# Chunk 5's product with w1 as seven block products, the tail's last product in two PSUM tiles, and a new order of steps

## The chip, the cores and the metric

The kernel runs on one core of one Trainium2 chip. The metric is the device time of one execution in microseconds (us). The core has five engines that run their own queues: TensorE (PE in the profile: matmuls, with PEld for its weight loads), VectorE (DVE), ScalarE (ACT), GpSimd (POOL) and SyncE (SP, which here only issues DMAs). Matmul results land in PSUM, eight banks of 512 float32 columns on 128 partitions; VectorE and ScalarE read them from there.

## The reference

Eight batches, eight heads, 576 tokens, 64 columns a head. An attention without a score matrix comes first, then a feed-forward block that multiplies two products:

```python
def _attn_ref(q, k, v):
    q_s = q - np.max(q, axis=-1, keepdims=True)
    q_s = np.exp(q_s)
    q_s = q_s / (np.sum(q_s, axis=-1, keepdims=True) + 1e-09)
    k_s = k - np.max(k, axis=2, keepdims=True)
    k_s = np.exp(k_s)
    k_s = k_s / (np.sum(k_s, axis=2, keepdims=True) + 1e-09)
    kv = np.einsum('bhsd,bhse->bhde', k_s, v)
    return np.einsum('bhsd,bhde->bhse', q_s, kv).astype(np.float32)

def _moe_ref(x, w1, w2, w3, w_out):       # x: 4608 x 512
    a = x @ w1                            # 512 x 1024
    b = x @ w2
    h = a * b @ w3                        # 1024 x 1024
    return (h @ w_out).astype(np.float32) # 1024 x 512
```

## The kernel before

The kernel folds w3 and w_out into one matrix W3O (1024 x 512) at its start, so that a chunk of tokens needs three products: with w2, with w1, and of their elementwise product `ab` with W3O.

**Chunks.** Chunk c (0 to 7) holds 512 of batch c's 576 tokens; chunk 8 holds the remaining 64 tokens of all eight batches (512 again). For each batch, `attention(b)` plans the softmax steps of k (`kmx`, `cba`, `cbx`, `cb`, `ksub`, `kexp`) and of q (`qmx`, `qsub`, `qexp`, `qsm`, `qeps`, `qrc`, `qn`), the copy of v to float16 (`vc`), the small product k'v (`kv`, read out by `kve`, `kvr`, `kv2`), a DMA transpose of q (`qd`), and the product that gives x transposed (`xm.b.0` and `xm.b.1` for the chunk, `xt` for the 64 other tokens). `xs.b.p.i` and `xts` move x from PSUM to SBUF. A name's first number is the batch or chunk; in `up`, `vp` and `vk` the first number is 0 for w1 and 1 for w2.

**Products with w1 and w2.** In chunks 0 to 5 an `up` step is a group of matmuls that fills one PSUM tile of the ring `pab` (four tiles): four matmuls of 512 columns (chunks 2 to 5), or eight of 256 (chunks 0 and 1). `bs` copies w2's result to SBUF, `ab` multiplies w1's result from PSUM with it (VectorE). In chunks 6 to 8 (the list `UPS`) each product is cut into 2 x 2 blocks and done with seven block products in place of eight: `vp.one.c.g.i`, i from 1 to 7, g for one of two halves of the columns, four matmuls of 256 columns each (`gate`, L923). They need sums of blocks: of the weights (`wd`, `gate_sum`) and of x (`xd`, `x_sum`); partial results are copied out (`vk`, `gkept`), and the four blocks come together in `bs` (w2), `as` and `ab` (w1). `UP1`, an empty list here, names chunks in which w1 alone is done that way; the code for it is there.

**Product with W3O.** In chunks 2 to 8 (the list `SEVEN`) it is done with seven block products too: `sp.c.i` (`product`, L1009), eight matmuls of 256 columns each, with sums of `ab` (`sa`, `sums_of`) and of W3O (`sT`), three copies (`kept`), and the output blocks `os.c.11`, `os.c.12`, `os.c.21`, `os.c.22` (`block`, L1033). Block products 2, 1 and 7 take a tile each from the ring `po` (two tiles), in chunk 8 from `pab`; 6, 5 and 3 add to 1's tile, 4 to 7's. `st` stores a block by a DMA on SP's queue (`store_block`, L1044). In chunk 8 (the list `FINE`) block product 4 is cut into `sp.8.40` and `sp.8.4`, each with one half of the tile, and the last block is added and stored in halves (`os.8.210`, `os.8.21`, `st.8.210`, `st.8.21`).

**Order.** There is no scheduler at run time. `ORDER` is a list of all steps, written out in the file; `Plan.run` (L48) emits them in that order, and each engine works off its own steps in that order, waiting for semaphores where data or a buffer is late. `PICKS` says for steps that can run on two engines which one does it. Large elementwise steps that read SBUF alone (`ksub`, `qsub`, `qn`, `sa`, `sT`, `wd`, `xd`, `ab` from SBUF, and `vc` on GpSimd) are marked as steps of a port: where the list goes from one engine to the other among them, `run` adds a wait, so that VectorE and GpSimd take turns on them in the order of the list. The loads of q, k and v from batch 2 on stand in SP's queue with the stores and the DMA transposes. v of batches 2 to 7 uses one input buffer (`turn_of`); the other one holds the weight sums of w1 later.

A step that takes a tile of a ring must stand behind the steps that free the tile's last holder (in `Plan.run`):

```python
ring, n = fifo[s["takes"]], self.rings[s["takes"]]
for old in range(len(ring) - n, len(ring) - n + s["slots"]):
    assert old < 0 or done.issuperset(given[ring[old]]), name
```

## Time and profile before

| | |
|---|---|
| median of 3 runs | 231.06 us (231.03 to 231.07) |
| the profiled execution | 231.18 us, its span 229.4 us |
| TensorE busy, granted clock | 220.8 us (96%), 0.997 |
| VectorE busy | 202.3 us (88%) |
| ScalarE busy | 146.3 us (64%) |
| GpSimd busy | 144.0 us (63%) |

The span goes from the first to the last instruction of the profiled execution; 1.8 us of its time lie outside. A row of a timeline gives start, length, engine, line, operation, output and inputs, and in brackets how long the engine had been idle and what ended that. Matmuls are pipelined, and their ends are modelled: the step from one start to the next is what a group costs, its length is longer. A row of a list of groups gives busy time, mean duration in ns, and the idle time before them. Tiles that share a buffer appear under the buffer's name: `v` in the tail is an output tile, `w` a block sum.

### The profile page before, as it was taken

Reading aid. Unit: us, or ns where it says so; the run is one execution under the profiler, and the core shown is the slowest. Engines: PE = TensorE matmul, PEld = TensorE weight load, DVE = VectorE, ACT = ScalarE, POOL = GpSimd, SP = SyncE. Lnnn points to the kernel's source line nnn. Section 1 sums busy time; section 2 is a strip of 40 time slices with the busy share of each in tenths; the row PEclk is TensorE's granted clock in tenths of the full one; section 3 lists DMA queues with packets and bytes.
Section 4 is the critical chain, followed back from the end, with each engine's and each line's share of the span. In section 5 each row is a group of like instructions: output and inputs, shape, how many; then the busy total and the mean of one; then the engine's idle time right before and its main releaser. Section 6 shows DMA issues by size and latency. Waiting matters only on the chain.

```text
span 229.4 us, 5579 instructions
## 1 busy us (share of the span) xinstructions
PE 220.8 (96%) x2239; PEld 149.1 (65%) x2239; DVE 202.3 (88%) x312; ACT 146.3 (64%) x277; POOL 144.0 (63%) x93
## 2 busy tenths in 40 slices
PE   7789999999999999999999999999999999999993
PEld 2345558865857644445666665664788788888882
DVE  1997769989896999999999799899989999899982
ACT  0536855479963999959947988448568453244431
POOL 8233247919999997984895894643199335729200
PEclk9999999999999999999999999999999999999998
DMA  6999999999999979999993867872804420041447
GB/s 202 220 309 213 293 261 264 315 381 294 398 307 208 376 275 238 299 237 275 294 366 101 165 137 193 324 140 46 184 1 91 95 62 1 3 91 38 102 95 225
DMA packets 42201, 46.56 MB, mean 203 GB/s; under 512 B 17088, under 2 KB 29888, under 8 KB 42176
## 3 DMA queue, kind: packets, MB, share of 16 engines
q1 hardware_dynamic: 34640, 34.48, 54.6%
q0 software_dynamic: 7536, 11.73, 21.9%
q8 instruction: 17, 0.28, 0.5%
q14 instruction: 8, 0.07, 0.1%
HBM read 38.80 MB, written 9.44 MB: 210 GB/s over the span
## 4 chain that ended last, share of the span: by engine, by line
PE 68%; DMA 20%; POOL 5%; DVE 3%; issue 2%; ACT 1%; POOLq 0%; DVEq 0%
PE pab L850 27%; PE po L1023 16%; PE pg L938 9%; PE pab L938 7%; DMA q<-in_q_dram 7%; DMA k<-in_k_dram 6%; DMA w1sb<-in_moe_w_dram 5%; PE pab L1023 3%; PE po L872 2%; DMA qT<-en 2%; POOL en L656 2%; POOL q L624 2%; PE pkv L579 2%; PE xm L704 1%; DVE qr L637 1%
## 5 line engine op out<-in xcount | busy, mean ns | idle before, releaser
L850 PE MATMUL pab<-x,w1sb 128*128 128x256 f16 (+1 forms) x256 | 49.5, 326 | 0.1
L850 PE MATMUL pab<-x,w2sb 128*128 128x256 f16 (+1 forms) x256 | 49.5, 326 | 0.0
L554 POOL TENSOR_TENSOR k<-k,cb 128x1152 f32<-128x1152 f32 x13 | 34.1, 2631 | 14.5 <-DVE w L1007 8.7
L850 PEld LDWEIGHTS <-w1sb 128*128 128x128 f16 x256 | 24.5, 98 | 14.9 <-issue 0.4
L850 PEld LDWEIGHTS <-w2sb 128*128 128x128 f16 x256 | 24.3, 98 | 15.1 <-issue 1.1
L865 DVE TENSOR_TENSOR ab<-pab,bsb 128x512 f16<-128x512 f32 x48 | 31.8, 676 | 1.7 <-ACT bsb L365 1.2
L624 POOL TENSOR_TENSOR q<-q,qm 128x1280 f32<-128x1280 f32 (+1 forms) x13 | 27.8, 2144 | 4.7 <-issue 2.3
L365 ACT CAST bsb<-pab 128x512 f16<-128x512 f32 x37 | 21.7, 586 | 12.5 <-PE pab L850 12.1
L656 POOL TENSOR_TENSOR en<-eq,qr 128x1024 f16<-128x1024 f16 (+1 forms) x12 | 25.3, 2123 | 6.0 <-ACT bsb L365 5.0
L619 DVE TENSOR_REDUCE qm<-q 128x20 f32<-128x1280 f32 (+1 forms) x16 | 21.3, 1340 | 3.7 <-DMA q<-in_q_dram 3.7
L637 DVE TENSOR_REDUCE qr<-eq 128x20 f32<-128x1280 f16 (+1 forms) x16 | 21.4, 1341 | 1.1 <-ACT eq L632 1.0
L632 ACT ACTIVATE eq<-q 128x1280 f16<-128x1280 f32 (+1 forms) x16 | 18.6, 1167 | 5.4 <-DVE q L624 3.9
L1023 PEld LDWEIGHTS <-w 128*128 128x128 f16 x192 | 18.6, 98 | 4.1 <-issue 0.4
L531 DVE TRANSPOSE_TENSOR_REDUCE kt<-k 128x72 f32<-128x2304 f32 x8 | 20.6, 2570 | 0.3 <-DMA k<-in_k_dram 0.3
L365 ACT COPY q<-pg 128x512 f32<-128x512 f32 x19 | 10.8, 586 | 13.9 <-PE pg L938 7.7
L1023 PEld LDWEIGHTS <-ab 128*128 128x128 f16 x168 | 16.4, 98 | 4.3 <-issue 1.0
L562 ACT ACTIVATE ek<-k 128x1152 f16<-128x1152 f32 x16 | 18.4, 1167 | 0.0
L1023 PE MATMUL po<-w 128*128 128x256 f16 x144 | 18.0, 273 | 0.0
L1007 POOL TENSOR_TENSOR w<-ab 128x1024 f16<-128x1024 f16 x5 | 10.6, 2123 | 9.7 <-PE pg L938 3.7
L500 PE MATMUL po<-wosb,w3T 128*128 128x512 f16 x64 | 15.3, 379 | 0.6 <-DMA wosb<-in_moe_w_out_dram 0.4
L872 PE MATMUL po<-W3O,ab 128*128 128x512 f16 x64 | 15.2, 379 | 0.0
L365 ACT CAST v<-v 128x1152 f16<-128x1152 f32 x12 | 13.6, 1155 | 1.1 <-DMA v<-in_v_dram 1.0
(145 smaller groups left out, 425.4 us busy)
## 6 DMA issues: line engine op xcount, KB each, us to landing
out_dram<-osb SPq DMA_DIRECT2D x56, 128.0 KB, 2.5
q<-in_q_dram SPq DMA_DIRECT2D x5, 1152.0 KB, 8.0
v<-in_v_dram SPq DMA_DIRECT2D x5, 1152.0 KB, 7.6
k<-in_k_dram SPq DMA_DIRECT2D x4, 1152.0 KB, 10.4
k<-in_k_dram POOLq DMA_DIRECT2D x3, 1152.0 KB, 14.2
v<-in_v_dram POOLq DMA_DIRECT2D x1, 1152.0 KB, 13.5
q<-in_q_dram SPq DMA_DIRECT2D x2, 576.0 KB, 6.5
k<-in_k_dram SPq DMA_DIRECT2D x2, 576.0 KB, 5.4
```

The costliest lines, as they stand in the source:

```text
L365: return [(nc.scalar.copy if eng == "ACT" else engine[eng].tensor_copy)(out=out, in_=in_)]
L531: dve.tensor_reduce(out=st["kt", b].rearrange("p h j e -> p (h j e)"), in_=kb.rearrange("p h j (e c) -> p (h j e) c", c=QD), axis=AX.X, op ...
L554: return [engine[eng].tensor_tensor(out=kb[:, two(hp), :, :], in0=kb[:, two(hp), :, :], in1=st["cb", b][:, two(hp), None, :].broadcast_to( ...
L619: dve.tensor_reduce(out=st["qm", b][:, :, j], in_=qb[:, :, j, :], axis=AX.X, op=ALU.max)
L624: return [engine[eng].tensor_tensor(out=qb[:, :, j, :], in0=qb[:, :, j, :], in1=st["qm", b][:, :, j, None].broadcast_to([P, HH, n, D]), op ...
L637: dve.tensor_reduce(out=st["qr", b][:, :, slice(*PARTS[p])], in_=st["eq", b, p], axis=AX.X, op=ALU.add)
L656: return [engine[eng].tensor_tensor(out=st["en", b][:, j, :, :].rearrange("p j h d -> p h j d"), in0=st["eq", b, p], in1=st["qr", b][:, :, ...
L850: nc.tensor.matmul(st["p", one, c, sub, u][:, a * (t1 - t0):(a + 1) * (t1 - t0)], lhsT=w[:, ct, fb * P:(fb + 1) * P], rhs=x()[:, ct, t0:t1 ...
L865: dve.tensor_tensor(out=st["ab", c][:, nf * u:nf * u + nf, t0:t1], in0=cut(st["p", 0, c, sub, u]), in1=cut(st["bsb", c, sub, u]), op=ALU.mult)
L872: nc.tensor.matmul(st["po", c, tb], lhsT=st["ab", c][:, ft, tb * P:(tb + 1) * P], rhs=W3O[:, ft, :], start=(ft == 0), stop=(ft == N_FT - 1))
L938: nc.tensor.matmul(st["pg", one, c, g, bank][:, a * 256:a * 256 + 256], lhsT=t[:, c0 + ct, f:f + P], rhs=r[:, r0 + ct, t0:t0 + 256], start ...
L1023: nc.tensor.matmul(st["ps", c, bank][:, tb * 256:tb * 256 + 256], lhsT=t[:, f0 + ft, t0 + tb * P:t0 + tb * P + P], rhs=r[:, g0 + ft, c0:c0 ...
```

## The change

- `UP1 = [5]`: in chunk 5 the product with w1 is done by `vp.0.5.g.i`, 14 block products of four 256-wide matmuls, with `xd.5.*`, `vk.0.5.*`, `as.5.*` and `ab.5.*`. The product with w2 stays whole but is cut by halves of the tokens (`up1`, L953): `up.1.5.sub.u`, eight matmuls of 256 columns each.
- In chunk 8 block product 7's tile becomes two tiles (two slots of `pab`): block products 7 and 4 write 128 tokens' half into each, and the block sums of `os.8.22`, `os.8.210` and `os.8.21` are done half by half.
- `st.8.210` is issued from ScalarE's queue; `st.8.21` stays on SP's.
- `ORDER` is new from behind `ab.1.1.1` (chunk 1's fifth multiplication) on, and 70 entries of `PICKS` name another engine. Among them from VectorE to GpSimd: `sT.2`, `sT.4`, `qn.3.1`, `qn.7.0`; `xs.6.0.0` and `xs.6.0.1` go from ScalarE to VectorE; `sa.7.3`, `sa.8.3`, `ab.8.0.0` and `ab.8.1.3` go to GpSimd, where `sa.7.2`, `sa.7.4`, `ab.8.1.2` and `ab.8.0.1` stand already. For chunk 5, `xd.5.1` and `ab.5.0.0` are on GpSimd, the other `xd`, all `as` and the other `ab` on VectorE, `vk` and `bs` on ScalarE.

```diff
-bs.1.1.1 xs.2.0.1 cbx.3 ab.1.1.1 v.3 cb.3 sT.3 up.1.1.1.2 qsub.3.0 sT.1 st.0.2 bs.1.1.2 up.0.1.1.2
...
-wd.1.4 st.3.11 kvr.6 os.4.11 os.4.21 kv2.6 xm.6.1 qrc.7.0 cbx.7 bs.5.0.5 xm.6.0 st.4.21 xs.6.1.0
-up.0.5.0.5 ab.5.0.4 sa.5.3 xs.6.1.1 xs.6.0.1 up.1.5.0.6 cb.7 xs.6.0.0 up.0.5.0.6 wd.0.2 qn.7.0
-vp.1.6.0.1 wd.0.4 vp.0.6.0.2 xd.6.1 vp.0.6.0.1 bs.5.0.6 ab.5.0.5 vk.1.6.0.1 xd.6.2 up.1.5.0.7 wd.1.3
...
-kv2.7 os.5.12 xm.7.1 xm.7.0 xts.6.0 ab.6.0.1 xs.7.1.0 as.6.0.3 xt.7 xs.7.1.1 ab.6.1.3 sp.6.1
-xs.7.0.1 xs.7.0.0 xd.7.3 xd.7.1 xd.7.2 ab.6.0.3 vp.1.7.0.1 ab.6.0.2 xts.7.0 xts.7.1 xts.6.1 sa.6.1
...
-st.7.21 sp.8.3 os.8.22 os.8.12 st.8.11 sp.8.40 st.7.12 st.8.22 os.8.210 sp.8.4 st.8.12 st.8.210
-os.8.21 st.8.21
+bs.1.1.1 xs.2.0.1 cbx.3 ab.1.1.1 sT.1 v.3 up.1.1.1.2 up.0.1.1.2 qsub.3.0 bs.1.1.2 cb.3 xm.2.1
...
+wd.0.4 kept.3.3 sp.3.3 up.1.4.0.5 os.3.22 bs.4.0.4 kvr.5 qd.5.1 cb.6 sp.3.4 vc.6.1 ab.4.0.3 bs.4.0.5
+qsub.7.0 qsm.6.0 os.3.12 st.2.21 up.0.4.0.5 sp.3.2 qeps.6.1 up.1.4.0.6 ab.4.0.4 up.0.4.0.6 kv2.5
+qexp.7.0 os.3.21 qd.5.0 ksub.6.0 ab.4.0.5 os.3.11 xm.5.0 bs.4.0.6 ksub.6.1 qmx.7.1 xm.5.1 xs.5.0.0
+k.7 ab.4.0.6 xs.5.1.1 xt.5 xs.5.0.1 xts.5.0 st.3.21 qsub.7.1 up.1.4.0.7 qeps.6.0 up.0.4.0.7 xs.5.1.0
+bs.4.0.7 qsm.7.0 qrc.6.1 ab.4.0.7 sp.4.1 v.7 xd.5.1 xts.5.1 up.1.5.1.0 kexp.6.1 vp.0.5.0.1
+vp.0.5.0.2 up.1.5.1.1 sa.4.3 kexp.6.0 vp.0.5.1.1 kept.4.1 st.3.11 wd.0.3 xd.5.3 qeps.7.0 qrc.6.0
+sa.4.1 sp.4.7 vk.0.5.0.1 bs.5.1.1 bs.5.1.0 xd.5.2 wd.1.3 wd.1.1 up.1.5.0.0 vp.0.5.1.2 vp.0.5.0.6
...
+kve.6 os.4.11 as.5.0.3 up.1.5.1.3 kvr.6 kv2.6 xm.6.0 os.4.21 xm.6.1 bs.5.1.2 bs.5.1.3 xs.6.1.0
+xs.6.1.1 xs.6.0.1 st.4.21 bs.5.0.2 vc.7.1 xs.6.0.0 sa.5.3 up.1.5.0.3 xd.6.3 vp.1.6.0.1 ab.5.1.2
...
+vp.0.6.1.4 kvr.7 kv2.7 os.5.12 qd.7.1 st.5.12 as.6.0.3 xt.6 ab.6.0.1 ab.6.1.2 xts.6.0 xm.7.1 st.5.22
+xm.7.0 xts.6.1 xs.7.1.1 xs.7.1.0 xs.7.0.1 xt.7 xs.7.0.0 sa.6.3 xd.7.1 sp.6.1 vp.1.7.0.1 xd.7.3
...
+as.8.0.2 vp.1.8.1.2 sa.7.3 ab.8.1.2 vp.0.8.1.7 ab.8.0.2 as.8.0.1 vk.0.8.1.2 vk.1.8.1.2 bs.8.0.1
+sa.7.2 vp.1.8.1.5 kept.7.1 vk.1.8.1.3 vp.0.8.1.5 vk.0.8.1.3 st.6.21 os.7.11 bs.8.1.3 ab.8.0.1 sp.7.6
+vp.1.8.1.3 vp.1.8.1.4 as.8.1.3 bs.8.1.1 vp.0.8.1.3 vp.0.8.1.4 bs.8.0.3 as.8.0.3 kept.7.2 ab.8.1.1
+sp.7.5 st.6.22 sa.7.4 ab.8.1.3 sp.7.7 ab.8.0.3 kept.7.3 sp.8.1 sa.8.1 sp.8.2 st.6.11 os.7.22
+kept.8.1 sp.7.4 sa.8.2 os.7.21 st.7.22 sp.8.6 os.8.11 sp.7.3 sa.8.3 kept.8.2 sp.8.5 st.7.11 os.7.12
+sa.8.4 sp.8.7 st.8.11 kept.8.3 os.8.22 sp.8.3 st.7.21 st.7.12 st.8.22 sp.8.40 sp.8.4 os.8.210
+os.8.12 st.8.12 st.8.210 os.8.21 st.8.21
...
@@ -357,7 +362,7 @@
     SEVEN = [2, 3, 4, 5, 6, 7, 8]
     UPS = [6, 7, 8]
     FINE = [8]
-    UP1 = []
+    UP1 = [5]
     SUBS = [[(0, 256), (256, 512)] if c in SPLIT else [(0, 512)] for c in range(B + 1)]
     engine = {"DVE": dve, "POOL": g_, "ACT": nc.scalar}
 
@@ -1011,6 +1016,9 @@
             fresh = i in (1, 2, 7)
             if fresh:
                 st["ps", c, bank] = p_o() if c < B else p_ab()
+                if i == 7 and c in FINE:
+                    st["ps", c, bank] = [st["ps", c, bank], p_ab()]
+            wide_ = i in (4, 7) and c in FINE
             a, w = st["ab", c], W3O
             left = {1: (a, 0, 0), 2: (a, 4, 0), 3: (mine[3], 0, 0), 4: (a, 4, 256),
                     5: (mine[0], 0, 0), 6: (mine[1], 0, 0), 7: (mine[2], 0, 0)}[i]
@@ -1020,11 +1028,13 @@
                 for ft in range(4):
                     t, f0, t0 = left
                     r, g0, c0 = right
+                    to = st["ps", c, bank][tb][:, 0:256] if wide_ else \
+                        st["ps", c, bank][:, tb * 256:tb * 256 + 256]
                     nc.tensor.matmul(
-                        st["ps", c, bank][:, tb * 256:tb * 256 + 256],
+                        to,
                         lhsT=t[:, f0 + ft, t0 + tb * P:t0 + tb * P + P],
                         rhs=r[:, g0 + ft, c0:c0 + 256],
-                        start=fresh and tb == 0 and ft == 0, stop=ft == 3, skip_group_check=True)
+                        start=fresh and (tb == 0 or wide_) and ft == 0, stop=ft == 3, skip_group_check=True)
 
         def kept(i, eng):
             st["kept", c, i] = work.tile([P, 512], F32, tag="w3T", name="kept", bufs=3)
@@ -1037,14 +1047,20 @@
                 copy(eng, st["osb", c, n], st["ps", c, 0])
                 return
             i, bank = {11: (1, 1), 22: (3, 2), 21: (2, 2)}[n]
-            cut = slice(0, 512) if part is None else slice(256 * part, 256 * part + 256)
+            if c in FINE and bank == 2:
+                for x in (0, 1) if part is None else (part,):
+                    cut = slice(256 * x, 256 * x + 256)
+                    dve.tensor_tensor(out=st["osb", c, n][:, cut], in0=st["ps", c, bank][x][:, 0:256],
+                                      in1=st["kept", c, i][:, cut], op=ALU.add)
+                return
+            cut = slice(0, 512)
             dve.tensor_tensor(out=st["osb", c, n][:, cut], in0=st["ps", c, bank][:, cut],
                               in1=st["kept", c, i][:, cut], op=ALU.add)
 
         def store_block(n, part=None):
             t0, c0 = n // 10 - 1, (n % 10 - 1) * 256
             if part is not None:
-                nc.sync.dma_start(
+                (nc.sync if part else nc.scalar).dma_start(
                     out=out.rearrange("(t p j) c -> p t j c", p=P, j=NJ)[
                         :, 2 * t0 + part, NM, c0:c0 + 256],
                     in_=st["osb", c, n][:, 256 * part:256 * part + 256])
@@ -1173,7 +1189,8 @@
                     continue
                 A(("sp", c, i), "PE", 0.87, lambda i=i: product(i),
                   needs + folded + [("sT", x) for x in range(1, 5)],
-                  takes=("po" if c < B else "pab") if taken else None)
+                  takes=("po" if c < B else "pab") if taken else None,
+                  slots=2 if i == 7 and c in FINE else 1)
             for i, after in ((1, 1), (2, 6), (3, 5)):
                 A(("kept", c, i), moves(C), 0, lambda eng, i=i: kept(i, eng), [("sp", c, after)],
                   takes="w3T")
```

139 lines of the change are left out of this document (65 added, 74 removed), and 81 rows, old and new, of the table PICKS.

## The prediction

> **What bounds the kernel now.** First the page: how busy each engine is over the span.
>
> ```profile
> span 229.4 us, 5579 instructions
> ## 1 busy us (share of the span) xinstructions
> PE 220.8 (96%) x2239; PEld 149.1 (65%) x2239; DVE 202.3 (88%) x312; ACT 146.3 (64%) x277; POOL 144.0 (63%) x93
> ```
>
> TensorE is busy 96% of the span. Is that all work, or does it wait? The list of waits, for TensorE alone, has six rows; the two left out above these are loads at the very start.
>
> ```profile
> PE pab L1023 <- DVE v L1041: 0.5, 1, 0.5
> PE xm L704 <- DMA qT<-en: 0.5, 1, 0.5
> PE po L500 <- DMA wosb<-in_moe_w_out_dram: 0.4, 1, 0.4
> PE po L1023 <- ACT x L369: 0.2, 1, 0.2
> ```
>
> The first row is the tail, which the change touches. Third, the busy time by stretches, from about the step where the two lists part (75.3 us, after `ab.1.1.1`) up to chunk 8's last products.
>
> ```profile
> core 0: us, PE busy (x) PEld busy (x) DVE busy (x) ACT busy (x) POOL busy (x), PEclk, DMA share, GB/s
> 75.30:137.76 62.46, 62.46 (x596) 34.62 (x597) 60.58 (x85) 53.14 (x106) 52.23 (x25) 1.00 0.88 249
> 137.76:181.10 43.34, 43.34 (x473) 30.56 (x475) 40.50 (x70) 27.90 (x55) 24.54 (x13) 1.00 0.56 137
> 181.10:199.67 18.57, 18.39 (x182) 15.90 (x183) 16.97 (x32) 9.05 (x19) 8.80 (x7) 1.00 0.15 31
> 199.67:217.60 17.93, 17.93 (x167) 16.04 (x165) 16.95 (x30) 8.43 (x15) 9.04 (x7) 1.00 0.34 74
> ```
>
> Over these 142.3 us TensorE lacks 0.18 us. So the time after 75 us is TensorE's work, and whatever shortens that work shortens the kernel, as long as nobody feeds it later. VectorE is close behind: 1.9, 2.8, 1.6 and 1.0 us idle, 7.3 in all. ScalarE and GpSimd have slack on the average (GpSimd 94.6 of 142.3), but GpSimd takes turns with VectorE on the port steps, in the order of the list.
>
> **The change part by part.** The sum is made against the profiled execution, 231.18 us, whose span is 229.4; the median of the runs shown is 0.12 lower. What differs by less than 0.2% (0.46 us) I call no change. "v in one buffer" is not in the diff: `turn_of` has it already. Cost: none.
>
> *Chunk 5's products.* Groups of eight 256-wide and of four 512-wide matmuls, side by side in the timeline:
>
> ```profile
> 76.84 1.04 PE L850 MATMUL pab<-x,w1sb 128*128 128x256 f16 x8
> 77.72 1.03 PE L850 MATMUL pab<-x,w2sb 128*128 128x512 f16 x4
> 78.58 1.03 PE L850 MATMUL pab<-x,w1sb 128*128 128x512 f16 x4
> 79.44 1.03 PE L850 MATMUL pab<-x,w2sb 128*128 128x512 f16 x4
> ```
>
> From start to start a 256-wide eight costs 0.88 us, a 512-wide four 0.86: 110 and 215 ns a matmul. Block products as chunks 6 to 8 have them, in the chain:
>
> ```profile
> 201.42 0.44 PE pab L938 x4
> 201.85 0.44 PE pg L938 x4
> 202.29 0.87 PE po L1023 x8
> ```
>
> One block product (4 matmuls) costs 0.435 us. With w1: eight groups of 0.86 (6.88 us) go, 2 x 7 block products (6.09) come: -0.79. With w2 the eight groups stay but are cut by token halves into 256-wide ones: 8 x 0.02 = +0.16. Net -0.63 us on TensorE, all of it on the path by the windows above. The weight loads rise by 56 (120 matmuls for 64); they lie under the matmuls, as the 0.435 row shows for the same form.
>
> By the Trainium skill ("TensorE: Matmul & The Clock Gate", section "Back-to-back issue gap") a sustained stream of weight load and matmul costs 81 ns a matmul at 128 columns and 131 at 512, so that half the width saves far less than half the time. By a straight line between them, an estimate from that page, 256 columns take 98 ns, and chunk 5 would go from 64 x 131 to 120 x 98 ns, 3.3 us longer in place of 0.63 shorter. The trace disagrees, with 215 and 110 ns, and the measurement decides.
>
> *The tail.* Its timeline:
>
> ```profile
> 224.57 0.60 PE L1023 MATMUL pab<-w,ab 128*128 128x256 f16 x4
> 224.57 0.42 PEld L1023 LDWEIGHTS <-ab 128*128 128x128 f16 x4 [0.15 <-issue]
> 224.63 0.58 ACT L365 COPY v<-pab 128x512 f32<-128x512 f32 x1 [1.16 <-PE pab L1023]
> 225.20 0.42 DVE L1041 TENSOR_TENSOR v<-pab,kept 128x256 f32<-128x256 f32 x1 [0.69 <-PE pab L1023]
> 225.68 0.60 PE L1023 MATMUL pab<-w,ab 128*128 128x256 f16 x4 [0.52 <-DVE v L1041]
> 225.68 0.31 PEld L1023 LDWEIGHTS <-ab 128*128 128x128 f16 x3 [0.69 <-issue]
> 225.71 1.40 SPq L1047 DMA_DIRECT2D out_dram<-v  x2
> 226.32 0.42 DVE L1041 TENSOR_TENSOR v<-pab,kept 128x256 f32<-128x256 f32 x1 [0.69 <-PE pab L1023]
> ```
>
> `sp.8.4` waits until VectorE has read the first half (`os.8.210`), because both halves lie in one tile. With two tiles and the new order it follows `sp.8.40` at 224.57 + 0.435 = 225.0 and ends at 225.61; `os.8.21` then starts at 225.65, when `os.8.210` ends, in place of 226.32: -0.67 us. The second tile takes a fourth slot of `pab`, whose holder two products back is long read. `os.8.22` becomes two adds of 0.42 for one: not on the path, since `sp.8.40` needs the first only. From the last add's end (226.74) to the span's end are 2.66 us of store, which stay. The store of the first half goes to ScalarE's queue, behind `os.8.12` (done 225.21). No row shows such a store. From below: on SP it would be issued at 225.71 and hold the queue for half of the 1.40, so the move saves up to 0.3. From above: it is issued 0.42 us ahead of the last store, so it must be slower than SP's by more than that to set the end, and if it were slower by a whole SP pair (1.40) it would cost 1.0. I take 0 beyond the -0.67, by the nearest row, SP's own.
>
> *The work around it.* w1's eight multiplications from PSUM become six additions and two multiplications of the same shape, six small multiplications, four sums of x and six copies. ScalarE gets the copies. By the picks VectorE gets five of the small multiplications and three sums, about 0.42 each as the small adds above: +3.4 us. The list gives as much back: from the parting step on, VectorE has 225 steps for 222, GpSimd 62 for 52. What that costs GpSimd:
>
> ```profile
> L554 POOL TENSOR_TENSOR k<-k,cb 128x1152 f32<-128x1152 f32 x13 | 34.1, 2631 | 14.5 <-DVE w L1007 8.7 <-DVE k L554 4.9 <-DVE cb L550 0.9
> L624 POOL TENSOR_TENSOR q<-q,qm 128x1280 f32<-128x1280 f32 x7 | 16.3, 2340 | 2.3 <-issue 2.3
> L656 POOL TENSOR_TENSOR en<-eq,qr 128x1280 f16<-128x1280 f16 x6 | 14.0, 2338 | 5.1 <-ACT bsb L365 5.0
> L624 POOL TENSOR_TENSOR q<-q,qm 128x1024 f32<-128x1024 f32 x6 | 11.5, 1915 | 2.4 <-DVE rc L600 1.6 <-DVE w L1007 0.8
> L656 POOL TENSOR_TENSOR en<-eq,qr 128x1024 f16<-128x1024 f16 x6 | 11.4, 1907 | 0.9 <-DVE qr L649 0.6 <-issue 0.4
> L1007 POOL TENSOR_TENSOR w<-ab 128x1024 f16<-128x1024 f16 x5 | 10.6, 2123 | 9.7 <-PE pg L938 3.7 <-DVE rc L600 3.3 <-DVE w L1007 2.7
> L993 POOL TENSOR_TENSOR ab<-ab,spare 128x512 f16<-128x512 f16 x5 | 5.7, 1155 | 2.6 <-DVE w L1007 1.9 <-DVE ab L986 0.7
> ```
>
> Net: two `sT` (2.12 each, as L1007), two `qn` (2.34, 1.91), six `ab` and two `xd` (1.155), one `vc` (about 1.15), less one `ksub` (2.63) and an `sa` and a `wd` (2.12): +12 us, 107 of 142. It still fits on the average, so the average costs nothing. Taken at nothing, cover and all: if a GpSimd step on the way to a product comes late, TensorE waits by just that. SP's queue keeps its loads and stores; `qd.6.0` and `qd.6.1` now stand close ahead of `xm.6`, but their `qn` come 9.9 and 9.0 us of products ahead (6.8 before).
>
> *The new list's seams.* Where a batch's x enters its chunk, products wait for fresh evictions. The only such wait now, in the chain:
>
> ```profile
> 181.08 0.20 PE pab L704 x6
> 181.30 0.28 ACT xtail L369
> 181.58 0.56 ACT x L369
> 182.18 1.03 PE po L1023 x8
> ```
>
> Here `sp.6.1` waits for `xs.7.1.0`, behind one `xts` (0.28) on ScalarE. The new list puts `xts.6.0` and `xts.6.1` ahead of it: about +0.25. At batch 6 the old list has three `up` groups between `xm.6.0` and `vp.1.6.0.1`, the new one only `up.1.5.0.3` (0.88), and both `xs.6.0` on VectorE, one after the other:
>
> ```profile
> L371 DVE TENSOR_SCALAR x<-xm 128x512 f16<-128x512 f32 x4 | 2.7, 686 | 2.0 <-PE xm L704 2.0
> ```
>
> From the start of `xm.6.0`: its results after 0.4 to 0.6 (a modelled group above is 0.60 long, its issue 0.435), two moves 1.37, so about 1.9; TensorE has two `xm` of some 0.25 (the chain's 0.20) and 0.88, 1.4. Wait 0.4 to 0.6; VectorE's `os.4.21` just ahead could add 0.69, an earlier start of VectorE could take it all away. I take 0.4. At batches 4 and 5 the same count comes out within 0.15 of even: 0.1 for both.
>
> Sum: 231.18 - 0.63 - 0.67 + 0.25 + 0.4 + 0.1 = 230.6 on the profiled execution, 230.5 on the median.
>
> **The rivals.**
> *No new waits.* VectorE's 7.3 us of slack would absorb the seams: 231.06 - 1.30 = 229.8. For it: TensorE lost only 0.18 us in 142 before. Against: the seams counted above.
> *The gain is eaten.* Small waits of 0.9 to 1.7 us in all: 231.1. The place I trust least is the end: `sa.7.3`, `ab.8.1.2`, `sa.7.2`, `ab.8.0.1`, `sa.7.4`, `ab.8.1.3` all on GpSimd (3 x 2.12 + 3 x 1.155), with `ab.8.0.2` and `ab.8.0.3` on VectorE (0.42 each) in their port order, 10.7 us ahead of `sp.8.2`, against 6.6 us of products from `sa.7.3`'s place (7 x 0.435 + 4 x 0.88). GpSimd must run 4.1 us ahead there; following its chain back I find about 4.4.
> *Slower: VectorE and GpSimd become the bound.* One mechanism: `qsub.7.0`, `ksub.6.0`, `ksub.6.1`, `qsub.7.1`, `xd.5.1` stand in one run on GpSimd (1.92 + 2 x 2.63 + 2.34 + 1.155 = 10.7), between `wd.0.4` and `sa.4.3` on VectorE, which `sp.4.7` needs: with `sa.4.3` (0.69 at most, as the move above) 11.4, against about 11.7 of products. VectorE late by more than 0.3 at `wd.0.4` delays TensorE one for one; over 1.3 us late, and the kernel is slower by more than 0.2%. Two us late gives 231.06 - 0.55 + 1.7 = 232.2. For it: 97% busy VectorE in the first stretch. Against: no wait of this kind before.
> *The store does not pay.* ScalarE's queue 1 us slower than SP's: 230.5 + 0.6 = 231.1.
> *Narrow matmuls cost their weight load.* If the 56 loads (0.42 for four, in the tail) lay bare: +5.9, 231.06 - 1.3 + 5.9 = 235.7. [...]
>
> **How the numbers follow.** Forecast (230.5) 0.45, no new waits 0.13, gain eaten 0.19, store 0.03, VectorE and GpSimd 0.18, weight loads 0.02. Faster 0.58, same 0.22, slower 0.20. The likeliest case alone reaches from 229.9 to 230.6 or so; the range must take in the gap-free case with the store's 0.3 (229.5) and most of the slower one (232.0), which leaves out less than 2 in 10.
>
> **What would show it.** Right: 14 block products of 0.44 in chunk 5, no TensorE wait on VectorE in the tail, last add 0.67 us nearer to `sp.8.40`; waits at `vp.1.6.0.1` and `sp.6.1` of about 0.4 each. Wrong: TensorE waiting for `w` of L1007 at `sp.4.7` or for `ab` at `sp.8.2`, VectorE without idle time before them; or ScalarE's store as the last thing to land.

## The result

The changed kernel takes 232.81 us (median; 231.78 to 233.14) beside 231.04 us for the kernel before (230.68 to 231.07) on the same chip: a ratio of 1.0067, 95% interval 1.0042 to 1.0092. It is slower, where 230.5 was forecast, and above the 232.0 up to which the range was to reach. The profiled execution took 233.14 us, with a span of 231.4; that of the kernel before took 231.18, with a span of 229.4. One run of the whole record, 235.26 us of e5_store_order_load, was disturbed: its ratio leaves that run out, its median does not.

On TensorE the change did in the main what was forecast. The waits of TensorE behind 75 us in the changed kernel (us in total, times, longest):

```profile
PE pg L943 <- ACT gkept L370: 0.6, 1, 0.6
PE pab L855 <- DVE ab L870: 0.3, 1, 0.3
PE po L1033 <- ACT x L374: 0.3, 1, 0.3
PE po L1033 <- DVE w L1012: 0.2, 1, 0.2
PE pg L943 <- DVE x L376: 0.2, 1, 0.2
```

The wait of the tail (0.5 us for VectorE) is gone, the one at `sp.6.1` has grown from 0.2 to 0.3, and four others of 0.2 to 0.6 us have come. TensorE is busy for 220.0 us in place of 220.8:

```profile
PE 220.0 (95%) x2295; PEld 154.8 (67%) x2295; DVE 200.8 (87%) x318; ACT 146.5 (63%) x274; POOL 155.6 (67%) x103
```

The timeline of its tail (start, length, engine, line):

```profile
224.81 1.04 PE L1033 MATMUL pab<-w,ab 128*128 128x256 f16 x8
225.01 0.58 ACT L370 COPY v<-pab 128x512 f32<-128x512 f32 x1 [1.16 <-PE pab L1033]
225.45 0.86 DVE L1053 TENSOR_TENSOR v<-pab,kept 128x256 f32<-128x256 f32 x2 [0.81 <-PE pab L1033]
225.91 0.38 ACTq L1063 DMA_DIRECT2D out_dram<-v  x1
```

`sp.8.40` and `sp.8.4` run as one group of eight, and the last add ends at 225.45 + 0.86 = 226.31, earlier even than the 226.74 of the kernel before. But the span ends 5.1 us behind that add, in place of 2.66. What lies there is SP's queue. First the kernel before, then the changed kernel (start, length from the first issue of the row to the end of the last):

```profile
212.84 9.43 SPq L1060 DMA_DIRECT2D out_dram<-k  x6
222.37 0.55 SPq L1053 DMA_DIRECT2D out_dram<-k  x1
223.02 1.26 SPq L1060 DMA_DIRECT2D out_dram<-v  x2
224.54 1.07 SPq L1053 DMA_DIRECT2D out_dram<-v  x2
225.71 1.40 SPq L1047 DMA_DIRECT2D out_dram<-v  x2
```

```profile
208.28 1.25 SPq L1076 DMA_DIRECT2D out_dram<-osb  x2
219.40 3.75 SPq L1076 DMA_DIRECT2D out_dram<-k  x4
223.26 0.54 SPq L1069 DMA_DIRECT2D out_dram<-k  x1
223.84 1.26 SPq L1076 DMA_DIRECT2D out_dram<-k  x2
225.20 1.25 SPq L1076 DMA_DIRECT2D out_dram<-v  x2
226.54 1.08 SPq L1069 DMA_DIRECT2D out_dram<-v  x2
227.71 0.45 SPq L1063 DMA_DIRECT2D out_dram<-v  x1
```

In the kernel before, `st.7.11` goes out at 212.84, as soon as its block is done, and the queue has gaps up to the end. In the changed kernel nothing is issued from 209.5 to 219.40. `st.7.11`, whose block was done at 213.71, stands behind `st.7.22` in the new list and waits with it; from 219.40 on issue follows issue with about 0.1 us or less between them, and the last store, ready at 226.31, is issued at 227.71. One of the issues takes three times as long as its neighbours, and the last store lands 2.7 us after its issue, where it took 1.7 in the kernel before. The instructions that wrote the output between 219 and 229 us in the changed kernel (duration in ns, least, median, most), and its landing times:

```profile
L1076 SPq DMA_DIRECT2D out_dram<-k x6: 595/606/1816, 219.4 to 224.5; - x6
...
DMA to landing us min/median/max: 2.3/2.6/3.9
```

And the stretches of 1 us at the end, first before, then after (the last two columns are the mean busy share of the 16 DMA engines and the GB/s that they moved):

```profile
225.00:226.00 1.00, 0.48 (x5) 0.29 (x3) 0.42 (x1) 0.21 (x1) 0.00 (x0) 1.00 0.98 268
226.00:227.00 1.00, 0.28 (x3) 0.00 (x0) 0.42 (x1) 0.00 (x0) 0.00 (x0) 1.00 1.01 351
227.00:228.00 1.00, 0.00 (x0) 0.00 (x0) 0.00 (x0) 0.00 (x0) 0.00 (x0) 0.92 0.83 285
```

```profile
223.00:224.00 1.00, 1.00 (x12) 0.90 (x10) 0.12 (x1) 0.58 (x1) 0.00 (x0) 1.00 0.20 51
227.00:228.00 1.00, 0.00 (x0) 0.00 (x0) 0.00 (x0) 0.00 (x0) 0.00 (x0) 1.00 0.97 262
228.00:229.00 1.00, 0.00 (x0) 0.00 (x0) 0.00 (x0) 0.00 (x0) 0.00 (x0) 1.00 0.99 334
229.00:230.00 1.00, 0.00 (x0) 0.00 (x0) 0.00 (x0) 0.00 (x0) 0.00 (x0) 0.51 0.98 341
```

In both kernels the DMA engines are full at the end, and in the changed one they stand nearly idle just ahead of it, at 223 to 224. So there were three suspects for the end, each with a letter in what was expected of the runs: the order in SP's queue (theory Q), the rate at which the DMA engines drain the stores (D), and the long issue, which turned out to begin with a load of TensorE's own instructions (L). Beside them stood the tail's edit or its store on ScalarE's queue (rival A) and TensorE's new waits (rival W).

### The profile page after: what moved, and what is told of

Its sections match the earlier page's. It is cut to its first block, busy times and chain, and to the rows that moved or that the text cites. A ratio compares the mean times of both kernels' runs of the same rounds, so it can differ in the third digit from the quotient of the medians.

```text
span 231.4 us, 5709 instructions
## 1 busy us (share of the span) xinstructions
PE 220.0 (95%) x2295; PEld 154.8 (67%) x2295; DVE 200.8 (87%) x318; ACT 146.5 (63%) x274; POOL 155.6 (67%) x103
## 4 chain that ended last, share of the span: by engine, by line
PE 69%; DMA 14%; DVE 6%; POOL 5%; ACT 2%; issue 2%; POOLq 0%; DVEq 0%; ACTq 0%
PE pab L855 20%; PE po L1033 15%; PE pg L943 11%; PE pab L943 8%; DMA w<-in_moe_w_dram 7%; DMA q<-in_q_dram 5%; PE po L505 4%; PE pab L963 3%; PE pab L1033 2%; PE po L877 2%; DMA qT<-en 2%; POOL en L661 2%; POOL q L629 2%; PE pkv L584 2%; DVE qm L624 1%
## 5 line engine op out<-in xcount | busy, mean ns | idle before, releaser
L855 PE MATMUL pab<-x,w1sb 128*128 128x256 f16 (+1 forms) x224 | 41.3, 318 | 0.3 <-DVE ab L870 0.3
L855 PE MATMUL pab<-x,w2sb 128*128 128x256 f16 (+1 forms) x224 | 41.3, 319 | 0.0
L559 POOL TENSOR_TENSOR k<-k,cb 128x1152 f32<-128x1152 f32 x12 | 31.4, 2628 | 8.7 <-DVE k L559 4.6
L661 POOL TENSOR_TENSOR en<-eq,qr 128x1024 f16<-128x1024 f16 (+1 forms) x14 | 29.5, 2120 | 9.5 <-DVE spare L926 4.9
L370 ACT CAST bsb<-pab 128x512 f16<-128x512 f32 x42 | 24.2, 588 | 12.4 <-PE pab L855 10.7
L855 PEld LDWEIGHTS <-w1sb 128*128 128x128 f16 x224 | 21.6, 98 | 12.0 <-issue 0.6
L855 PEld LDWEIGHTS <-w2sb 128*128 128x128 f16 x224 | 21.3, 98 | 12.1 <-issue 1.0
L870 DVE TENSOR_TENSOR ab<-pab,bsb 128x512 f16<-128x512 f32 x40 | 26.4, 672 | 1.1 <-ACT bsb L370 1.0
L370 ACT COPY q<-pg 128x512 f32<-128x512 f32 x15 | 8.6, 588 | 12.7 <-PE pg L943 12.7
L943 PEld LDWEIGHTS <-v 128*128 128x128 f16 x128 | 12.5, 98 | 1.5
```

The costliest lines, as they stand in the source:

```text
L370: return [(nc.scalar.copy if eng == "ACT" else engine[eng].tensor_copy)(out=out, in_=in_)]
L559: return [engine[eng].tensor_tensor(out=kb[:, two(hp), :, :], in0=kb[:, two(hp), :, :], in1=st["cb", b][:, two(hp), None, :].broadcast_to( ...
L661: return [engine[eng].tensor_tensor(out=st["en", b][:, j, :, :].rearrange("p j h d -> p h j d"), in0=st["eq", b, p], in1=st["qr", b][:, :, ...
L855: nc.tensor.matmul(st["p", one, c, sub, u][:, a * (t1 - t0):(a + 1) * (t1 - t0)], lhsT=w[:, ct, fb * P:(fb + 1) * P], rhs=x()[:, ct, t0:t1 ...
L870: dve.tensor_tensor(out=st["ab", c][:, nf * u:nf * u + nf, t0:t1], in0=cut(st["p", 0, c, sub, u]), in1=cut(st["bsb", c, sub, u]), op=ALU.mult)
L943: nc.tensor.matmul(st["pg", one, c, g, bank][:, a * 256:a * 256 + 256], lhsT=t[:, c0 + ct, f:f + P], rhs=r[:, r0 + ct, t0:t0 + 256], start ...
```

## The experiments

All profiles are compared on two stretches. **Middle** runs from the start of the 541st matmul, at about 57 us, to that of the 15th last one, which lies in `sp.8.3`; it holds chunk 5 and every seam of the new list. **End** runs from there to the end of the span. Where a warm-up has more matmuls, the count begins that many later. The 541st matmul lies ahead of where the two lists part: the first matmul that differs is the 808th, at 81 us. What lies ahead of the middle is the same program in both, but for the three kernels with another warm-up (e5, e6, e8), and its length differs by up to 1 us from execution to execution. Each kernel has one profile, so middle and end are of one execution each. Times are medians; the difference is against the kernel before on the same chip at the same time. The changed kernel was run on the first chip alone, so the others are compared with it by difference and ratio. The ratio is not that of the medians, and the two can differ.

| kernel | time, us | difference | ratio (95%) | middle | end |
|---|---|---|---|---|---|
| before | 231.04 | | | 167.13 | 5.74 |
| after | 232.81 | +1.77 | 1.0067 (1.0042 to 1.0092) | 167.79 | 7.31 |
| e1_store_order | 231.91 | +0.63 | 1.0036 (1.0016 to 1.0057) | 166.69 | 6.18 |
| e2_before_tail | 231.18 | -0.10 | 0.9992 (0.9975 to 1.0010) | 167.18 | 5.60 |
| e3_before_tail_sp | 231.04 | -0.24 | 0.9990 (0.9979 to 1.0001) | 166.94 | 5.73 |
| e4_after_sp_store | 232.58 | +1.30 | 1.0062 (1.0042 to 1.0082) | 167.18 | 7.30 |
| e5_store_order_load | 232.69 | +1.64 | 1.0059 (1.0041 to 1.0078) | 167.11 | 6.05 |
| e6_before_load | 231.61 | +0.56 | 1.0023 (1.0002 to 1.0044) | 166.77 | 5.97 |
| e7_tail_less_store | 230.91 | -0.14 | 0.9997 (0.9984 to 1.0011) | 166.93 | 5.54 |
| e8_seams | 232.72 | +1.67 | 1.0070 (1.0048 to 1.0092) | 166.51 | 6.02 |
| e9_two_stores | 231.39 | +0.26 | 1.0025 (1.0007 to 1.0043) | 167.09 | 5.75 |
| e10_two_stores_seams | 231.73 | +0.60 | 1.0026 (1.0007 to 1.0045) | 166.93 | 5.91 |
| e11_tail_less_812 | 230.40 | -0.73 | 0.9968 (0.9954 to 0.9982) | 166.95 | 5.05 |
| e12_before_less_812 | 231.08 | -0.05 | 0.9989 (0.9977 to 1.0002) | 167.10 | 5.80 |
| e13_tail_712_early | 230.89 | -0.29 | 0.9988 (0.9975 to 1.0002) | 166.96 | 5.41 |
| e14_after_load | 232.15 | +0.97 | 1.0055 (1.0042 to 1.0068) | 167.31 | 6.18 |
| e15_before_712_early | 231.14 | -0.04 | 1.0002 (0.9991 to 1.0013) | 167.00 | 5.73 |

### One store moved in the queue

```diff
-sp.8.2 st.6.11 os.7.22
+sp.8.2 st.6.11 st.7.11 os.7.22
...
-kept.8.2 sp.8.5 st.7.11 os.7.12
+kept.8.2 sp.8.5 os.7.12
```

> The changed kernel with one step of the list moved: the store st.7.11 stands right behind st.6.11 on SP's queue, ahead of st.7.22, as in the list before. Theory Q (the loss is SP's in-order queue: 13 store issues in a row from 219.40 to 228.16, while os.7.11 had been done at 213.71): two issues of 0.65 us leave that stretch, so the last store can be issued right behind its add (226.4 in place of 227.71): 1.3 us less, up to 2.3 if it then also lands in the 1.72 us of before and not in 2.74: 230.5 to 231.5, likeliest 231.2. Rival A (the two PSUM tiles or the store on ScalarE's queue lengthen the end): no change, 232.5 to 233.1. Rival W (TensorE's waits in the new list are the loss): no change, 232.5 to 233.1. On the one issue of 1.8 us at 221.33: if it belongs to a place in SP's stream of instructions, it stays on about the same count of instructions, now the second half of st.7.22.

The end is 1.13 us shorter than in the changed kernel, and the time 231.91, far from the 232.5 and more of the rivals, though above the 230.5 to 231.5 of theory Q. One word of the list was 1.14 of the 1.77 us by the medians, and a little under half of the loss by the ratios (1.0036 beside 1.0067). The queue of this kernel:

```profile
219.29 1.25 SPq L1076 DMA_DIRECT2D out_dram<-k  x2
221.90 0.42 SPq L1069 DMA_DIRECT2D out_dram<-k  x1
222.37 1.33 SPq L1076 DMA_DIRECT2D out_dram<-k  x2
223.80 1.25 SPq L1076 DMA_DIRECT2D out_dram<-v  x2
```

No issue takes 1.8 us any more. But SP stands from 220.54 to 221.90: it waits for `os.8.11`, since the new list has `st.8.11` ahead of `st.7.21`, whose block is done earlier. That is the second thing in the order. Rival W fell: the waits behind 160 us are all still there in this profile, and the kernel is faster.

### The second store moved too

```diff
-sp.8.7 st.8.11 kept.8.3 os.8.22 sp.8.3 st.7.21 st.7.12
+sp.8.7 st.7.21 st.8.11 kept.8.3 os.8.22 sp.8.3 st.7.12
```

This stands on top of the edit above.

> The changed kernel with two steps of the list moved: st.7.11 behind st.6.11 as in e1_store_order, and st.7.21 ahead of st.8.11, as in the list before. In e1_store_order SP's queue stood from 220.55 to 221.90 waiting for os.8.11 while os.7.21 was done. Theory Q: 256 KB more are gone by then, and from the fifteenth last matmul to the end there are 5.6 to 5.8 us, as in e2_before_tail and e3_before_tail_sp, in place of 6.18 in e1_store_order and 7.31 in the changed kernel: 0.4 to 0.6 less than e1_store_order, 1.3 to 1.6 less than the changed kernel, 231.2 (230.9 to 231.6) beside a kernel before of 231.05. If the two PSUM tiles or ScalarE's queue lengthened the end: 231.7 or more.

231.39, and an end of 5.75: that of the kernel before, within 0.01. With the stores in the old order the whole loss at the end is gone, with the two PSUM tiles and ScalarE's queue still in place. Theory Q held, and rival A fell. The time is not yet that of the kernel before: the ratio, 1.0025, is clear of 1, and 5 of the 12 runs took 231.9 us or more, where 2 of 33 of the kernel before did. e6_before_load below, with the old list and as many matmuls as the changed kernel, scatters likewise (4 of 12). The profile is of a run of 231.38, so what the longer ones lose isn't shown.

### ScalarE's queue

```diff
-                (nc.sync if part else nc.scalar).dma_start(
+                nc.sync.dma_start(
```

> The changed kernel with the store of the first half (st.8.210) back on SP's queue. Theory Q: one more issue of 0.45 to 0.65 in a queue that is full to the last store: 0.4 to 0.7 slower than the changed kernel, 233.2 to 233.5. Rival A with ScalarE's queue as its cause: faster than the changed kernel, 232.3 or less. Rival W: no difference.

Neither slower, as theory Q had it, nor faster, as rival A: a ratio of 1.0062 beside 1.0067, and an end of 7.30 beside 7.31. One more issue stands in the full queue, and the last store is issued at 228.20 in place of 227.71, but it lands at 230.50 in place of 230.45. Theory Q was too simple by half: what comes last is not the issue but the landing. The Trainium skill's page "DMA: Bandwidth & Descriptors" says under "Issuing engines are not separate DMA queues": "DMAs initiated by the scalar, sync or gpsimd engine will ultimately run on the same 16 DMA engines and interleave with each other, regardless of the engine that started them." The trace agrees: half a microsecond less on SP's queue bought 0.05 at the end.

### The tail's edit alone, in the kernel before

The edit of `product`, `block` and `slots` as in the change, `sp.8.4` moved behind `sp.8.40` in the old list:

```diff
-sp.8.40 st.7.12 st.8.22 os.8.210 sp.8.4 st.8.12
+sp.8.40 sp.8.4 st.7.12 st.8.22 os.8.210 st.8.12
```

> The kernel before, with the tail's edit alone: two PSUM tiles for the last products, sp.8.4 right behind sp.8.40, the first half's store on ScalarE's queue. Theory Q: the old list keeps SP's queue free at the end, so the 0.67 us of the last add come through whole: 231.05 - 0.67 = 230.4 (230.2 to 230.7). Rival A: the store on ScalarE's queue or the second tile costs at the end: 231.0 or more.

> As the kernel before with the tail's edit, but the first half's store stays on SP's queue (225.7 to 226.15), with the last store right behind it. Theory Q: the last add ends at 226.07, the last store is issued at about 226.2: 0.1 more than with ScalarE's queue, 230.5. Rival A with the store as its cause: faster than with ScalarE's queue by 0.3 or more.

Both intervals reach 1: 0.10 and 0.24 us by the medians, where 0.67 was expected, and it makes no difference that can be told which queue takes the first half. The profile of e3_before_tail_sp has the last store issued at 226.27, and it takes 2.2 us to land in place of 1.7. Its last stretches:

```profile
226.00:227.00 1.00, 0.00 (x0) 0.00 (x0) 0.00 (x0) 0.00 (x0) 0.00 (x0) 1.00 1.02 353
227.00:228.00 1.00, 0.00 (x0) 0.00 (x0) 0.00 (x0) 0.00 (x0) 0.00 (x0) 1.00 0.88 303
```

The DMA engines are full from behind the last product to the end. That gave theory D: the end comes when the stores have drained.

### Less data at the end

In `store_block`, on top of e3_before_tail_sp; `st.7.12` left out, then `st.8.12`, and `st.8.12` in the kernel before:

```diff
-            for i in range(2):
+            for i in range(0 if (c, n) == (B - 1, 12) else 2):
```

```diff
             if c == B:
+                if n == 12:
+                    return
```

> As e3_before_tail_sp (the kernel before with the two PSUM tiles, all stores on SP's queue), with the store st.7.12 left out: that block of the output is not written. Theory D: in e3_before_tail_sp the DMA engines are full from 223 to 228 and the last store lands 2.2 us after its issue in place of 1.72, so the 0.5 us that the tail's products gain are not seen; without those 256 KB the last store lands 1.72 us after its issue again: 0.4 to 0.6 less, 230.5 to 230.7. Rival (the tail's two tiles gain nothing for another cause): no change, 231.0 to 231.2.

> As e3_before_tail_sp (kernel before with the two PSUM tiles, all stores on SP's queue), with the store st.8.12 left out: that block of the output is not written. Theory D (the last 512 KB, st.8.12, st.8.210 and st.8.21, leave at some 0.36 us per 128 KB, so that the end cannot come earlier than st.8.12's landing and two such pieces): without st.8.12 the last store lands 1.7 to 1.9 us after its add, which is 0.67 earlier than in the kernel before: 0.6 to 0.8 less than e3_before_tail_sp and 0.5 to 0.7 less than e12_before_less_812. If the tail's edit gained nothing on TensorE or VectorE: as e12_before_less_812.

> The kernel before with the store st.8.12 left out: that block of the output is not written. Theory D: its last store comes 0.67 us later than with the two tiles and lands 1.72 us after its issue with or without st.8.12: 0 to 0.2 less than the kernel before, 230.9 to 231.05. If DMA's drain alone sets the end in both: 0.5 or more less than the kernel before.

The first missed: 230.91, no gain over e3_before_tail_sp by the ratios, and 0.19 us in the end stretch. Its profile says why: `st.8.12` lands at 227.24, `st.8.210` at 227.60, `st.8.21` at 227.95. The last three stores still come one upon another, 0.36 us for 128 KB. The other two settle it. With `st.8.12` gone, the tail's edit is worth 231.08 - 230.40 = 0.68 us by the medians, 0.75 in the end stretch and 0.2% (0.5 us) by the ratios; the forecast was 0.67. With `st.8.12` it is worth 0.1 to 0.24. The last store of e11_tail_less_812:

```profile
225.27 0.84 SPq L1058 DMA_DIRECT2D out_dram<-v  x2
...
DMA to landing us min/median/max: 1.8/1.8/1.8
```

And leaving the store out of the kernel before gains nothing (231.08 beside 231.13), since there the last store is issued 0.8 us later, counted from the 15th last matmul (3.10 beside 2.30), and finds the engines free (0.28 busy from 227 to 228). The bound can be read from the kernel before: `st.8.12` landed at 227.62, two pieces of 128 KB behind it take 2 x 0.36, which is 228.34. The last store landed at 228.49. So by this account 0.15 us was all there was to gain; in e3_before_tail_sp the same sum, 227.77 + 0.72, gives 228.49, and that is when it landed.

### A store moved ahead

`sp.7.3` and `sp.8.2` change places, with `os.7.12` on ScalarE, in e3_before_tail_sp and in the kernel before:

```diff
-sp.7.7 os.7.22 sa.8.2 sp.8.2 sa.8.4 sp.8.1
+sp.7.7 sp.7.3 os.7.22 os.7.12 sa.8.2 sa.8.4 sp.8.1
...
-sp.8.6 st.7.22 os.7.21 sa.8.3 sp.7.3 kept.8.2
+sp.8.6 st.7.22 st.7.12 os.7.21 sa.8.3 sp.8.2 kept.8.2
```

> As e3_before_tail_sp (kernel before with the two PSUM tiles, stores on SP's queue), with sp.7.3 and sp.8.2 changing places, so that the block 12 of chunk 7 is ready and stored some 3 us earlier, behind st.7.22, and the block 11 of chunk 8 about 0.6 us later; os.7.12 on ScalarE. Theory D: the DMA engines have less left when the last blocks come, and the tail's gain comes through in part: 0.3 to 0.6 less than e3_before_tail_sp, 230.4 to 230.7 (beside a kernel before of 231.05). If the amount of late stores doesn't matter: as e3_before_tail_sp, 230.9 to 231.1.

> The kernel before with the same two products in changed places, without the tail's edit. Theory D: the last add comes 0.67 later, so the drain is hardly what ends it: 0 to 0.2 less than the kernel before, 230.85 to 231.05. If the changed places alone gain (for TensorE or VectorE): as much less as e13_tail_712_early is than e3_before_tail_sp.

By the profile as expected: an end of 5.41 with the tail's edit (5.73 without the swap) and 5.73 without it. By the time the first missed, 230.89 where 230.4 to 230.7 was expected, and it can't be told apart from e3_before_tail_sp: a ratio of 0.9988 (0.9975 to 1.0002) beside 0.9990. By the median it is the fastest version that writes all of the output; against the changed kernel it is clearly faster, against the kernel before that is not shown.

### The long issue: TensorE's instructions

The changed kernel has 18 packets of 16 KB on the queue `q8 instruction`, the kernel before 17 (part 3 of the pages; first before, then after):

```profile
q8 instruction: 17, 0.28, 0.5%
```

```profile
q8 instruction: 18, 0.29, 0.5%
```

That is one load in 2 x 2239 / 17 = 263 and in 2 x 2295 / 18 = 255 instructions of TensorE, matmuls and weight loads together. The change adds 112 such instructions, and with them comes the eighteenth load, at 221.36; the long issue began at 221.33. Three experiments move the loads:

```diff
-    "begin": 17, "pf.5.0": 6,
+    "begin": 47, "pf.5.0": 6,
...
-    def fill(n):
+    def fill(n, cols=512):
...
-            nc.tensor.matmul(idle, lhsT=zero[:, 0:P], rhs=zero, start=True, stop=True)
+            nc.tensor.matmul(idle[:, 0:cols], lhsT=zero[:, 0:P], rhs=zero[:, 0:cols], start=True, stop=True)
...
-        fill(FILL["begin"])
+        fill(FILL["begin"], 176)
```

> The changed kernel with st.7.11 moved up, as in e1_store_order, and 30 more pairs of weight load and matmul in the warm-up ahead of the first data (47 narrow matmuls in place of 17 wide ones, the same columns in all). Theory L: the stall at 221.3 in the changed kernel (an issue of 1.82 us) and at 220.5 to 221.9 in e1_store_order is a load of TensorE's own instructions, 16 KB on queue q8, an eighteenth one that the kernel before has not, and it delays the stores in flight. 60 more instructions bring it about 3.2 us earlier, to about 218.3, where no store is under way: 0.7 to 1.2 us less than e1_store_order, 230.7 to 231.2. Theory D (the last stores come out at the rate of the DMA engines, whatever stalls): some of it, 0 to 0.7 less. Theory Q alone (SP's queue): no change, 231.9.

> The kernel before with 56 more pairs in the warm-up (73 narrow matmuls in place of 17 wide ones): as many instructions on TensorE as the changed kernel has. Theory L: an eighteenth load comes at about 221.5, into the stores of the end, and the kernel gets slower by 0.4 to 1.2 us, with an issue of about 1.8 us or a late landing behind 221: 231.7 to 232.4. Theories Q and D without L: no change, 231.2.

In the second it is 73 and 112, in the kernel before. The third is the changed kernel with chunk 4's `up` products cut in two:

```diff
-                    for ct in range(N_CT):
-                        nc.tensor.matmul(st["p", one, c, sub, u][:, a * (t1 - t0):(a + 1) * (t1 - t0)],
-                                         lhsT=w[:, ct, fb * P:(fb + 1) * P], rhs=x()[:, ct, t0:t1],
-                                         start=(ct == 0), stop=(ct == N_CT - 1))
+                    for h in range(2 if c == 4 else 1):
+                        n = 256 if c == 4 else t1 - t0
+                        for ct in range(N_CT):
+                            nc.tensor.matmul(st["p", one, c, sub, u][:, (a + h) * n:(a + h + 1) * n],
+                                             lhsT=w[:, ct, fb * P:(fb + 1) * P],
+                                             rhs=x()[:, ct, t0 + h * n:t0 + h * n + n],
+                                             start=(ct == 0), stop=(ct == N_CT - 1))
```

> The changed kernel, with the matmuls of chunk 4's up products cut in two (256 wide in place of 512): 32 more pairs of weight load and matmul between 85 and 120 us, some 0.2 us of products. List and stores as in the changed kernel. Theory L: the last load of TensorE's instructions comes 64 instructions, some 3.4 us, earlier, at 218.0 in place of 221.4, ahead of the stretch of stores; no store's issue takes 1.8 us, and from the fifteenth last matmul to the end there are 6.1 to 6.4 us in place of 7.31: 0.7 to 1.2 less than the changed kernel, 231.7 to 232.2. Theory Q alone (order and number of stores on SP's queue): no change, 232.6 to 233.0.

The last one moves the load and leaves the list and the order of the stores as they are in the changed kernel. By its profile theory L held: an end of 6.18 in place of 7.31. By the times it is not settled: 232.15, against its own kernel before 0.8 us less than the changed kernel by the medians, but a ratio of 1.0055 beside 1.0067, from five and six runs, whose intervals overlap. The last load came at 215.1, earlier than the 218.0 expected, and the issues of the same six instructions were:

```profile
L1079 SPq DMA_DIRECT2D out_dram<-k x6: 595/605/615, 219.0 to 222.9; - x6
```

None is long, and the stretch in which the DMA engines of the changed kernel are 0.20 busy is full:

```profile
223.00:224.00 1.00, 1.00 (x11) 0.90 (x10) 0.47 (x2) 0.49 (x1) 0.00 (x0) 1.00 1.00 318
```

In e4_after_sp_store, where the load stayed (221.53), the long issue stayed (1.68 us at 221.39). So the order of the stores and the load are not two sums to be added: moving `st.7.11` or moving the load gives back 1.13 us of the end, either alone. A queue with gaps takes the load without harm (5.75 in e9_two_stores); a full one without the load beside it is 0.43 longer than that, one with it 1.56.

The first one missed, 232.69 in place of 230.7 to 231.2, though its end (6.05) was as short as theory L had it. It moved the early loads too, and one of them came at 51.9 us, into the transpositions of batch 1, where it took 2.35 us. TensorE then waited, where e1_store_order had waited 0.23:

```profile
56.11 0.41 PE L709 MATMUL xm<-qT,kv 64*64 64x256 f16 x8 [1.32 <-DMA qT<-en]
```

The same wait (1.33) stands in e8_seams, where the load came at 54.03 and took 1.07. That the load caused it fits in time and isn't shown by itself. The second, with an eighteenth load at 222.0 in the kernel before, was slower by 0.23% (0.02 to 0.44), at the low end of what was expected. In its profile one store under way landed 3.35 us after its issue, where 2.4 is usual, and the end grew by 0.23 us, but the start, which its other warm-up had changed, came out 0.44 longer too and the middle 0.36 shorter, so it bears theory L out only in part.

### The new list's waits

```diff
-as.6.1.2 vk.1.6.1.1 qrc.7.1 vp.0.6.0.3
+as.6.1.2 vk.1.6.1.1 qrc.7.1 kept.5.1 vp.0.6.0.3
...
-vk.1.6.1.2 kept.5.1 vp.1.6.1.5 sp.5.6 vk.1.6.1.3
+vk.1.6.1.2 sp.5.6 vp.1.6.1.5 vk.1.6.1.3
...
-xts.6.1 xs.7.1.1 xs.7.1.0 xs.7.0.1
+xs.7.1.1 xs.7.1.0 xts.6.1 xs.7.0.1
```

In e8_seams on top of e5_store_order_load, in e10_two_stores_seams on top of e9_two_stores.

> As e5_store_order_load, with two of TensorE's waits taken out by the order: kept.5.1 ahead of vp.0.6.0.3 and sp.5.6 ahead of vp.1.6.1.5 (the wait of 0.58 us at 172.4), and xts.6.1 behind xs.7.1.0 (the wait of 0.29 us at 182.7). If the waits of the new list count whole at the end: 0.6 to 0.8 less than e5_store_order_load. If the drain of the stores hides them: 0 to 0.2 less.

> As e9_two_stores, with the waits at 172.4 (0.58) and 182.7 (0.29) made shorter by the order: kept.5.1 ahead of vp.0.6.0.3, sp.5.6 ahead of vp.1.6.1.5, xts.6.1 behind xs.7.1.0. In e8_seams these two fell from 0.87 to 0.4 in all, and the stretch from the parting of the lists to the fifteenth last matmul was 0.6 shorter than in e5_store_order_load. If the end follows the products: 0.5 to 0.6 less than e9_two_stores, 230.7 (230.3 to 231.0). If the drain of the stores holds the end: as e9_two_stores.

The waits went from 0.6 and 0.3 to 0.2 and 0.2, and the middle became 0.60 shorter in the one pair (0.23 of it a wait at 115 us that only e5_store_order_load has) and 0.16 in the other. The times show none of it: 1.0070 beside 1.0059 and 1.0026 beside 1.0025, each within 0.2%. In the second pair the end grew by the 0.16 that the middle had lost. Whether the seams are worth anything to the time stays open.

## Why the prediction was wrong, step by step

**Chunk 5's products: right.** -0.63 was forecast on TensorE. Over the middle it is busy 0.65 us less, with 56 matmuls more (first before, then after: length, TensorE's busy time, clock, DMA share, GB/s):

```profile
56.53:223.66 167.13, 166.48 (x1685) 1.00 0.66 178
```

```profile
56.26:224.05 167.79, 165.83 (x1741) 1.00 0.63 175
```

The 0.8 us of the whole span have the tail's joined groups in them. The block products run one every 0.44 us:

```profile
142.02 0.60 PE L943 MATMUL pg<-x,w1sb 128*128 128x256 f16 x4
142.46 0.60 PE L943 MATMUL pab<-x,w1sb 128*128 128x256 f16 x4
142.90 1.04 PE L963 MATMUL pab<-x,w2sb 128*128 128x256 f16 x8
```

No weight load shows between them: the rival of the bare weight loads, with its 5.9 us, fell.

**The seams: more than forecast, and in other places.** Forecast were +0.4 at `vp.1.6.0.1`, +0.25 at `sp.6.1` and 0.1 for batches 4 and 5, 0.75 in all. Measured were 0.20, 0.11 (0.29 for 0.18) and a wait of 0.58 at `vp.1.6.1.5` that was not foreseen: a copy of `vk` whose buffer `as.6.0.2` still held. These 0.89 stand in the profiles of e1, e4 and e9. In that of the changed kernel 0.52 of waits for VectorE at 107 and 114 us come on top, 1.41 in all. Products and seams together were forecast at +0.12. The middle is 167.02 in the mean of the eight profiles with the old list and the old warm-up (166.93 to 167.18), 167.19 in the four with the new list's products unaltered (166.69 to 167.79): +0.17, with a spread that is too wide to confirm 0.12. That the new waits take all that chunk 5's new form gains is borne out by the two sums, -0.65 and at least +0.89. The middle is also part of the loss in the changed kernel's own profile: of the 1.96 us by which the changed kernel's span is longer, 0.66 lie in the middle and 1.57 in the end, and the start is 0.27 shorter.

**The tail's products: right, and worth nothing.** From the start of `sp.8.40` to the last add's end there were 226.74 - 224.57 = 2.17 us and are 226.31 - 224.81 = 1.50: the 0.67 of the forecast. What failed is the sentence behind it, "From the last add's end (226.74) to the span's end are 2.66 us of store, which stay." They were taken as a latency that follows the add. They are the end of a queue: the last 512 KB land one upon another, as the DMA engines move them, and the kernel before was already within 0.15 us of that. The 0.68 between e12_before_less_812 and e11_tail_less_812, and the 0.1 to 0.24 of e2 and e3, by the medians, show it.

**SP's queue: the step that cost most.** "SP's queue keeps its loads and stores" was true of their number and not of their order. `st.7.11` behind `st.7.22` kept SP's queue empty from 209.5 to 219.40 and full from there on; `st.8.11` ahead of `st.7.21` made it wait once more when the first was mended. Moving the two words back is worth 1.5 us by the medians (+1.77 to +0.26), 0.42% (1.0 us) by the ratios and 1.56 in the end stretch. The prediction followed the new list for four engines and not for the one that has no work of its own.

**The load of instructions: not in the prediction.** The 56 added matmuls and their weight loads were costed on TensorE alone. They also bring an eighteenth load of its instruction stream, and it fell into the full queue. By the end stretch, the order of the stores without it costs about 0.4 us (6.18 in e14_after_load against 5.75), and the load without that order nothing (5.75 with the load at 221.3 in e9_two_stores) or 0.23 (e6_before_load). The share of the load rests on these profiles; the times don't show it.

**The rivals.** The forecast of the slower case, 232.2, was near the time, but by another mechanism: no wait at `sp.4.7` or `sp.8.2` came. GpSimd did become busier where it was feared, 33.24 of the 35 us from 75 to 110 against 28.27, and the two waits for VectorE at 107 and 114 us lie there or just behind; they came in the profile of the changed kernel, one of them (0.2) in that of e5_store_order_load, and none in the six others with that list, in which GpSimd is just as busy (33.20 to 33.47). What brings them is open. "The store does not pay" was right in its result and wrong in its reason: ScalarE's queue is not shown to be slower than SP's (e2 and e3 can't be told apart), and moving the store changed nothing at the end (e4). The 1.40 us that the prediction took for a pair of SP's issues are two issues of 0.44 and 0.34 with 0.62 between them, in which SP waits for the last add; its bounds for the store came from that misread row, but nothing in the sum hung on them.

## What to carry to other kernels

At the end of a kernel, compute the time at which the stores can have drained (the landing of the one before, plus bytes at the rate that the last rows show) before counting a product that ends earlier as a gain; here 0.15 of 0.67 us was to be had. When a list of steps is rewritten, read it for the queue that only issues transfers too: a store that stands behind one that is ready later waits with it, the DMA engines stay idle meanwhile, and its bytes are added to those of the end. Adding instructions to an engine moves the moments at which its program is loaded; such a load can fall into a stretch where transfers are dense, so look for it on the queues of kind `instruction` before taking a long issue or a late landing for the kernel's own.
